# Attention beside an ELU feed-forward network: scores of two units by quarters of the array

## Chip, cores and metric

One Trainium2 chip, one NeuronCore. The metric is the device time of the whole kernel in microseconds (us), the median of several executions. Engines are named as in the profile: PE (TensorE matmul) and PEld (its weight loads), DVE (VectorE), ACT (ScalarE), POOL (GpSimd), SP (SyncE, which only issues transfers here).

## What is computed

The reference, cut to what matters (batch 4, 8 heads, 768 positions, head size 64, all float32):

```python
k_sum = k.reshape(B, H, nb, 32, D).max(axis=3)          # 24 blocks of 32 positions
v_sum = v.reshape(B, H, nb, 32, D).mean(axis=3)
scores_l = where(|i - j| < 16, scale * q @ k.T, -1e9)
scores_s = scale * q @ k_sum.T + log(32)
a = softmax(concat([scores_l, scores_s]))
x = (a @ concat([v, v_sum]))                            # as [3072 tokens, 512]
h = x @ w_in                                            # 512 -> 2048
out = where(h > 0, h, exp(min(h, 0)) - 1) @ w_out       # 2048 -> 512
```

## The kernel before

**Feed-forward.** The 3072 tokens are worked in 6 chunks of 512, and the 2048 hidden features in 16 strips of 128, so there are 96 slots, numbered n (chunk c = n // 16, strip f = n % 16). In each slot PE does `layer1(c, f)` (12 matmuls of 128x128 weights against 512 columns, L499) and then `layer2` of the slot before (12 matmuls of the same size, L527). Each product is split into a rounded and a remaining part (xh, xl and gh, gl), which is why there are three matmuls for each 128x128 block. Between the layers ACT takes the exponential (L505), DVE makes the ELU of it (L509, L510), ACT rounds it to gh (L516) and POOL makes the rest gl (L517).

**Attention.** A unit is a third of one batch's sequence (256 positions, four windows of 64) for one pair of heads. A window's 64 queries see 96 neighbouring keys (its own 64 and 16 on each side) and the 24 block maxima, 120 columns in all (`KC`). The first two thirds of batch 0 are done by `first_units()` ahead of the slots. The other 40 units u are spread over the slots of the chunks before the one that uses them, one unit in two slots. Chunk 0 holds units 0 to 7, chunks 1 to 4 hold units 8 to 39, chunk 5 holds none.

- `unit_scores(u)` (L459 to L463), in an even slot between the two layers: four matmuls, one for each window, on the whole array. The weights are `qbd`, a block-diagonal tile: the first head's 64x64 queries in rows and columns 0 to 63, the second head's in 64 to 127, zeros elsewhere. Two DMAs (L398) lay q there. Float32 matmuls leave two records each in the trace, so a unit shows x8.
- `lowest` (DVE, L130) adds the mask to four windows and finds the extremum, `exps` (ACT, L137) takes the exponentials and their sums, `normalize` takes reciprocals on DVE (L142, L143) and scales on POOL (L144).
- `unit_transposes(u)` (L149), at the end of the even slot after the scores' own: four transposes into PSUM, and an ACT copy to `pt` (L478).
- `unit_values(u)` (L156), at the end of the next odd slot: eight matmuls (x16 in the trace) of 120x64 weights, one for each window and head, the two heads in two column halves of the array. `take_x` then moves the result to xh on ACT (L169) and xl on DVE (L170).

**Order.** Chunk 0 runs with the order on every engine as written. From chunk 1 on, only PE and SP keep the written order (L639); the order on DVE, ACT and POOL is chosen when the program is built. PSUM has eight banks: two for h, four for the outputs of layer 2, and a0 and a1, which all of attention shares; `bank(c)` (L443) gives a0 in chunk 0 and then a0 and a1 in turn. `load_unit` (L393) brings a unit's q, keys and values by DMA from SP; q has two buffers, keys and values have one for each pair of heads. The 24 means of v are summed by `means` (L450), four matmuls in four column quarters of the array, three times in the run, and once by `sums` in `first_units` (L315).

Of the kernel before, what the change touches and what calls it, by code (L numbers as in the profile page):

```python
# [17 lines left out]
F32 = mybir.dt.float32  # L18
# [8 lines left out]
P = 128  # L27
# [3 lines left out]
QW = 64  # L31
KB = QW + 2 * E
UW = 4
UT = UW * QW
# [4 lines left out]
def attn_elu_ffn(ctx: ExitStack, tc: tile.TileContext, qT, kT, vT, v, w_in, w_out, out):  # L39
# [81 lines left out]

    ks_all, vs_all = {}, {}

    def lowest(th, s_ps, sm):

        mx = att.tile([P, UW, 1], F32, tag="mx", name="mx", bufs=4)
        for t in range(UW):
            w = th * UW + t
            m = mask[:, 0 if w == 0 else 2 if w == NTH * UW - 1 else 1, :]
            nc.vector.tensor_tensor_reduce(out=sm[:, t, :], in0=s_ps[:, t, :], in1=m, scale=-scale, scalar=3.0e38,  # L130
                                           op0=ALU.add, op1=ALU.min, accum_out=mx[:, t, :])
        return mx

# [12 lines left out]
    def transposes(sm, tag, bufs=1):  # L146
        t_ps = psum.tile([P, UW, P], F32, tag=tag, name="t_ps", bufs=bufs)
        for t in range(UW):
            nc.tensor.transpose(t_ps[0:KC, t, :], sm[:, t, :], ident)  # L149
        return t_ps  # L150

    def values(v_t, w0, pt, tag):
        o_ps = psum.tile([P, UT], F32, tag=tag, name="o_ps")
        for t in range(UW):
            for h in range(2):
                nc.tensor.matmul(o_ps[h * D:(h + 1) * D, t * QW:(t + 1) * QW],  # L156
                                 v_t[0:KC, w0 + t, h * D:(h + 1) * D], pt[0:KC, t, h * QW:(h + 1) * QW],
                                 start=True, stop=True)
        return o_ps

# [229 lines left out]

    units = [(third, p) for third in range(2, NTH * B) for p in range(NP)]

    def load_unit(u):  # L393
        third, p = units[u]
        b, th = divmod(third, NTH)
        q_t = qbd[u % 2]
        for h in range(2):
            nc.sync.dma_start(  # L398
                out=q_t[h * D:(h + 1) * D, :, h * D:(h + 1) * D],
                in_=qT[b, p, h * D:(h + 1) * D, th * UT:(th + 1) * UT].rearrange("d (t q) -> d t q", q=QW))  # L400
        lo = 1 if th == 0 else 0
        hi = UW - 1 if th == NTH - 1 else UW
        src = kT[b, p]
        nc.sync.dma_start(out=kw[p][:, lo:hi, 0:KB],
                          in_=bass.AP(tensor=src.tensor, offset=src.offset + (th * UW + lo) * QW - E,
                                      ap=[[S, P], [QW, hi - lo], [1, KB]]))
        vsrc = v[b, :, p * P:(p + 1) * P]
        nc.sync.dma_start(out=vw[p][0:KB, lo:hi, :],
                          in_=bass.AP(tensor=vsrc.tensor, offset=vsrc.offset + ((th * UW + lo) * QW - E) * row,
                                      ap=[[row, KB], [QW * row, hi - lo], [1, P]]))  # L410
        if th == 0:
            nc.sync.dma_start(out=kw[p][:, 0, E:KB], in_=src[:, 0:KB - E])
            nc.sync.dma_start(out=vw[p][E:KB, 0, :], in_=vsrc[0:KB - E, :])
            put_maxima(b, p)
        if th == NTH - 1:
            nc.sync.dma_start(out=kw[p][:, UW - 1, 0:KB - E], in_=src[:, S - KB + E:S])
            nc.sync.dma_start(out=vw[p][0:KB - E, UW - 1, :], in_=vsrc[S - KB + E:S, :])
# [20 lines left out]
        for i, n in enumerate(got):  # L438
            nc.vector.tensor_reduce(out=dst[:, p, i * m:(i + 1) * m], in_=n, axis=AX.X, op=op)

    banks = {"n": 0}

    def bank(c):  # L443

        if c == 0:
            return "a0"
        banks["n"] += 1
        return f"a{banks['n'] % 2}"

    def means(b, c):  # L450
        ps = psum.tile([P, P], F32, tag=bank(c), name="vsps")
        for p in range(NP):
            nc.tensor.matmul(ps[p * BLK:(p + 1) * BLK, :], vst_all[b][:, p, :], ident, start=True, stop=True,
                             tile_position=(0, p * BLK))
        return lambda: nc.scalar.mul(out=vs_all[b], in_=ps, mul=1.0 / BLK)
# [2 lines left out]

    def unit_scores(u, c):  # L459
        p = units[u][1]  # L460
        s_of[u] = psum.tile([P, UW, KC], F32, tag=bank(c), name="s")
        for t in range(UW):
            nc.tensor.matmul(s_of[u][:, t, :], qbd[u % 2][:, t, :], kw[p][:, t, :], start=True, stop=True)  # L463

    def unit_low(u):
        sm_of[u] = att.tile([P, UW, KC], F32, tag="sm", name="sm")
# [2 lines left out]
    def unit_exps(u, low):  # L469
        z_of[u] = exps(sm_of[u], low)  # L470

    def unit_norm(u):
        normalize(sm_of[u], z_of.pop(u))

    def unit_transposes(u, c):
        t_ps = transposes(sm_of.pop(u), bank(c))
        pt_of[u] = att.tile([P, UW, P], F32, tag="pt", name="pt", bufs=1)
        return lambda: nc.scalar.copy(out=pt_of[u][0:KC], in_=t_ps[0:KC])  # L478

    def unit_values(u, c):  # L480
        third, p = units[u]
        if third % 2 == 0 and p == 0:
            new_x(third // 2)
        o_ps = values(vw[p], 0, pt_of.pop(u), bank(c))
        return lambda: take_x(o_ps, third, p)


    gs = {}
# [73 lines left out]
    def slot_a(n, c):  # L562

        u, odd = divmod(n, 2)
        if not odd and u + 1 < len(units):
            unit_scores(u + 1, c)
            if u + 2 < len(units):
                load_unit(u + 2)
        for b, first in first_of.items():
            if n == 2 * first - 1:  # L570
                means(b, c)()
            p, late = divmod(n - (2 * first - 1), 2)
            if 0 <= p < NP and not late:
                put_means(b, p, vw[p])

    def slot_b(n, c):
        u, odd = divmod(n, 2)
        return (unit_values if odd else unit_transposes)(u, c) if u < len(units) else lambda: None

    def begin_next():  # L580

# [8 lines left out]
    with tc.manual_schedule(engines=set(engines.values())):  # L590
        late = first_units()

        sums_at = {2: [(1, 0)], 3: [(0, 0)], 4: [(1, 1)], 5: [(0, 1), (1, 2)], 6: [(1, 3)], 7: [(0, 2)], 8: [(0, 3)]}
        got = {}
        new_summaries(1)
        e = None
        this = begin_next()
        for n in range(NF):
            u, odd = divmod(n, 2)

            h_ps = layer1(0, n)
            next(this, None)
            ahead = begin_next()
            if n > 0:
                split(0, n - 1, e)
            next(this, None)
            if n > 0:
                evacuate()
            list(late)
            if not odd:  # L610
                unit_norm(u)
            for i, p in sums_at.get(n, []):
                summary(1, p, (kT, vT)[i], got.pop((i, p)))
            slot_a(n, 0)
            for i, p in sums_at.get(n + 2, []):
                got[i, p] = load_summary(1, p, (kT, vT)[i], spares[i][p])
            load_more(12 + 2 * n)

            late, this = this, ahead
            next(this, None)  # L620
            ahead = begin_next()
            e = exp_of(h_ps)
            next(this, None)
            list(late)
            if not odd:
                low = unit_low(u + 1)
            elu(e, h_ps)
            if odd:
                unit_exps(u + 1, low)
            if n > 0:  # L630
                layer2(0, n - 1)
            late, this = this, ahead
            evacuate = slot_b(n, 0)
        list(late)
        split(0, NF - 1, e)
        evacuate()
        unit_norm(NF // 2)

    with tc.manual_schedule(engines={engines["PE"], engines["SP"]}):  # L639
        for n in range(NF, NCH * NF):  # L640
            c, f = divmod(n, NF)
            u, odd = divmod(n, 2)
            h_ps = layer1(c, f)
            e = exp_of(h_ps)
            turn = elu(e, h_ps)
            split(c, f, e)
            slot_a(n, c)
            if not odd and u + 1 < len(units):
                unit_exps(u + 1, unit_low(u + 1))
                unit_norm(u + 1)  # L650
            for b, first in first_of.items():
                p = n - (2 * first - 8)
                if p == 0:
                    new_summaries(b)
                for q, src in ((p, kT), (p - 2, vT)):
                    if 0 <= q < NP:
                        got = load_summary(b, q, src)
                        with tc.issue_after(turn):
                            summary(b, q, src, got)
            layer2(*divmod(n - 1, NF))  # L660
            slot_b(n, c)()
        layer2(NCH - 1, NF - 1)
# [37 lines left out]
```

## Time and profile before

| | us |
|---|---|
| median of 3 runs | 657.42 (657.16 to 658.16) |
| the profiled execution | 658.07 |
| its span, first to last instruction | 656.3 |
| PE busy | 639.7 (97%) |
| ACT, DVE, POOL busy | 275.6, 265.7, 245.3 |
| mean granted clock of PE | 0.99 of full speed |

A row of the timeline gives the start of a group of instructions, the time from its first start to its last end, the engine, the line, what is written and read, the tile of weights (rows*columns), the moving operand and the count. Starts are the safe part of a matmul's row: its end is modelled and overlaps the next one's start, so what a matmul costs is read from one start to the next.

### The profile page before, as it was taken

How to read it: one execution, taken by the hardware profiler on the slowest of the kernel's cores; microseconds unless marked ns; L12 is line 12 of the kernel's file. 1: busy time of each engine (PE TensorE's matmuls, PEld its weight loads, DVE VectorE, ACT ScalarE, POOL GpSimd, SP SyncE). 2: the span in 40 equal slices, each digit the busy share in tenths (PEclk: the TensorE clock that was granted, in tenths of full speed). 3: DMA queues.
4: the chain of work that ended last, by engine and by line, in shares of the span. 5: the costliest groups of instructions: out<-in, count | busy, mean ns of one | idle time of the engine just before them, and what ended most of it. 6: DMA issues, size and time to landing. Idle time of an engine off the chain costs nothing.

```text
span 656.3 us, 10774 instructions
## 1 busy us (share of the span) xinstructions
PE 639.7 (97%) x3916; PEld 523.8 (80%) x3916; DVE 265.7 (40%) x856; ACT 275.6 (42%) x750; POOL 245.3 (37%) x263
## 2 busy tenths in 40 slices
PE   8859999999999999999999999999999999999997
PEld 7648878888888878888888888888888888888885
DVE  7868887633224533322233543222322231322222
ACT  6757667644334333343344333433443343322222
POOL 5768989843222322232223232322232222222221
PEclk9969999999999999999999999999999999999999
DMA  9999965114122514121112551211321100100001
GB/s 315 208 317 351 308 212 167 33 36 125 32 56 80 151 34 134 36 60 38 32 35 72 171 137 38 70 32 33 97 64 31 32 1 1 64 1 1 0 1 64
DMA packets 86324, 60.24 MB, mean 92 GB/s; under 512 B 46464, under 2 KB 78464, under 8 KB 86272
## 3 DMA queue, kind: packets, MB, share of 16 engines
q1 hardware_dynamic: 82960, 53.66, 29.4%
q10 hardware_dynamic: 3312, 5.90, 2.4%
q8 instruction: 31, 0.51, 0.3%
q14 instruction: 21, 0.17, 0.1%
HBM read 52.46 MB, written 6.29 MB: 90 GB/s over the span
## 4 chain that ended last, share of the span: by engine, by line
PE 94%; DMA 2%; DVE 2%; ACT 1%; POOL 0%; SPq 0%; issue 0%; DVEq 0%
PE h L499 41%; PE o L527 40%; PE s L463 5%; PE o_ps L156 4%; PE t_ps L149 3%; DMA v<-in_v_dram 1%; DMA raw_w<-in_w_in_dram 1%; DMA raw_w<-in_w_out_dram 1%; DVE sm L130 1%; PE idle L227 1%; ACT sm L137 0%; PE s L290 0%; DVE sh L110 0%; DVE cv L113 0%; POOL raw_w L103 0%; DVE ks L276 0%
## 5 line engine op out<-in xcount | busy, mean ns | idle before, releaser
L499 PE MATMUL h<-xh,w 128*128 128x512 f32 x768 | 262.8, 403 | 0.0
L517 POOL TENSOR_TENSOR gl<-e,gh 128x512 fp32r<-128x512 f32 x96 | 123.9, 1290 | 205.3 <-issue 109.6
L527 PE MATMUL o<-w,gh 128*128 128x512 f32 x768 | 196.4, 394 | 0.0
L499 PEld LDWEIGHTS h<-xh,w 128*128 128x128 f32 x768 | 145.3, 189 | 31.2
L527 PEld LDWEIGHTS o<-w,gh 128*128 128x128 f32 x768 | 141.2, 188 | 28.2 <-issue 0.6
L499 PE MATMUL h<-xl,w 128*128 128x512 f32 x384 | 150.9, 393 | 0.0
L509 DVE TENSOR_SCALAR e<-e 128x512 f32<-128x512 f32 x96 | 45.1, 469 | 254.2 <-ACT e L505 254.1
L505 ACT ACTIVATE e<-h 128x512 f32<-128x512 f32 x96 | 57.4, 598 | 210.9 <-PE h L499 210.0
L144 POOL TENSOR_TENSOR sm<-sm,z 128x480 f32<-128x480 f32 x48 | 47.5, 990 | 157.0 <-ACT gh L516 130.9
L527 PE MATMUL o<-w,gl 128*128 128x512 f32 x384 | 105.3, 389 | 0.0
L516 ACT CAST gh<-e 128x512 fp32r<-128x512 f32 x96 | 59.0, 615 | 72.9 <-DVE e L510 71.6
L137 ACT ACTIVATE sm<-sm,mx 128x120 f32<-128x120 f32 x192 | 73.5, 385 | 26.5 <-DVE mx L130 26.5
L527 PEld LDWEIGHTS o<-w,gl 128*128 128x128 f32 x384 | 72.0, 188 | 15.2 <-POOL gl L517 0.2
L499 PEld LDWEIGHTS h<-xl,w 128*128 128x128 f32 x384 | 72.9, 190 | 13.0
L510 DVE SCALAR_TENSOR_TENSOR e<-h,e 128x512 f32<-128x512 f32 x96 | 66.2, 690 | 2.2
L170 DVE TENSOR_TENSOR xl<-o_ps,xh 128x256 fp32r<-128x256 f32 x48 | 20.0, 423 | 61.4 <-ACT xh L169 61.4
L118 POOL TENSOR_TENSOR w<-cv,w 128x512 fp32r<-128x512 f32 x32 | 42.4, 1325 | 6.7 <-ACT w L117 5.8
L463 PEld LDWEIGHTS s<-kw,qbd 128*128 128x128 f32 x320 | 41.8, 191 | 3.7 <-DVE xl L170 0.7
L130 DVE CUSTOM_DVE_ANT_0 sm<-s,mask 128x120 f32<-128x120 f32 x192 | 42.2, 277 | 1.8 <-PE s L463 1.7
L463 PE MATMUL s<-kw,qbd 128*128 128x120 f32 x320 | 41.9, 274 | 0.6 <-DVE xl L170 0.6
L149 PE MATMUL t_ps<-ident,sm 128*120 128x128 f32 x192 | 29.3, 276 | 8.5 <-DVE mx L130 6.8
L137 ACT ACTIVATION_READ_ACCUMULATOR sm<-sm,mx 128x1 f32 x192 | 36.1, 188 | 0.0
(66 smaller groups left out, 361.1 us busy)
## 6 DMA issues: line engine op xcount, KB each, us to landing
raw_w<-in_w_in_dram SPq DMA_DIRECT2D x16, 512.0 KB, 6.3
raw_w<-in_w_out_dram SPq DMA_DIRECT2D x16, 512.0 KB, 6.1
qbd<-in_qT_dram SPq DMA_DIRECT2D x80, 64.0 KB, 2.3
out_dram<-ot ACTq DMA_DIRECT2D x20, 256.0 KB, 3.8
kw<-in_kT_dram SPq DMA_DIRECT2D x28, 144.0 KB, 5.9
vw<-in_v_dram SPq DMA_DIRECT2D x28, 144.0 KB, 2.9
n<-in_kT_dram SPq DMA_DIRECT2D x16, 192.0 KB, 2.5
n<-in_vT_dram SPq DMA_DIRECT2D x16, 192.0 KB, 2.6
```

The lines of the kernel that those rows point to most:

```text
L130: nc.vector.tensor_tensor_reduce(out=sm[:, t, :], in0=s_ps[:, t, :], in1=m, scale=-scale, scalar=3.0e38, op0=ALU.add, op1=ALU.min, accum_o ...
L137: nc.scalar.activation(out=sm[:, t, :], in_=sm[:, t, :], func=AF.Exp, bias=mx[:, t, :], scale=-1.0, accum_out=z[:, t, :])
L144: nc.gpsimd.tensor_tensor(out=sm, in0=sm, in1=z.broadcast_to([P, UW, KC]), op=ALU.mult)
L149: nc.tensor.transpose(t_ps[0:KC, t, :], sm[:, t, :], ident)
L463: nc.tensor.matmul(s_of[u][:, t, :], qbd[u % 2][:, t, :], kw[p][:, t, :], start=True, stop=True)
L499: nc.tensor.matmul(h_ps, w[:, a, cols], bb[:, cc, :], start=(k == 0), stop=(k == 3 * NCC - 1))
L505: nc.scalar.activation(out=e, in_=h_ps, func=AF.Exp)
L509: nc.vector.tensor_scalar(out=e, in0=e, scalar1=1.0, scalar2=-1.0, op0=ALU.min, op1=ALU.add)
L510: top = nc.vector.scalar_tensor_tensor(out=e, in0=h_ps, scalar=0.0, in1=e, op0=ALU.max, op1=ALU.add)
L516: nc.scalar.copy(out=gh, in_=e)
L517: nc.gpsimd.tensor_tensor(out=gl, in0=e, in1=gh.bitcast(F32), op=ALU.subtract)
L527: nc.tensor.matmul(o_acc[c][s], a[:, s * P:(s + 1) * P], w[:, bb, :], start=first and f == 0, stop=last and f == NF - 1)
```

## The change

Chunk 0 stays as it was, but that it no longer scores unit 8. From there on, units go by twos, and one pair has four slots. `scores_of_two(u)` runs at the end of slot n = 2u - 1, after `layer2`: 16 matmuls with 64x64 weights, each on a quarter of the array: the row half is the head, the column half is the window's parity. Each head has a PSUM bank of its own (a0, a1). q is loaded as it lies, in one DMA, without the zeros. The transposes of the two units follow at the ends of the next two slots, and `values_of_two` does the values of both in one run at the end of the last slot. The masks of the first and last window now hold for one half of the partitions, so two halves are copied over once. `pt` gets two buffers. The number of operations on DVE, ACT and POOL for a unit is the same.

The diff, without the lines that only pass names on:

```diff
     def lowest(th, s_ps, sm, two=False):
...
+            s_t = s_ps[t % 2][:, t // 2, :] if two else s_ps[:, t, :]
+            nc.vector.tensor_tensor_reduce(out=sm[:, t, :], in0=s_t, in1=m, scale=-scale, scalar=3.0e38,
...
+    def values(v_t, w0, pt, tag=None, o_ps=None, two=False):
...
+                                 pt[0:KC, t // 2 * 2 + h, t % 2 * QW:(t % 2 + 1) * QW] if two else
+                                 pt[0:KC, t, h * QW:(h + 1) * QW],
...
+    def q_flat(u):
+        return qbd[u % 2].rearrange("p t k -> p (t k)")[:, 0:UT]
...
+        if u >= NF // 2:
+            nc.sync.dma_start(out=q_flat(u), in_=qT[b, p, :, th * UT:(th + 1) * UT])
+        for h in range(2 if u < NF // 2 else 0):
...
+    def scores_of_two(u):
+        s_ps = [psum.tile([P, UW, KC], F32, tag=f"a{h}", name="s") for h in range(2)]
+        for k in range(2):
+            for i in range(UW // 2):
+                for h, g in ((0, 0), (1, 0), (0, 1), (1, 1)):
+                    rows = slice(h * D, (h + 1) * D)
+                    w = 2 * i + g
+                    nc.tensor.matmul(s_ps[h][g * QW:(g + 1) * QW, 2 * k + i, :],
+                                     q_flat(u + k)[rows, w * QW:(w + 1) * QW], kw[units[u + k][1]][rows, w, :],
+                                     start=True, stop=True)
+        for k in range(2):
+            sm_of[u + k] = att.tile([P, UW, KC], F32, tag="sm", name="sm")
+            low = lowest(units[u + k][0] % NTH, [s[:, 2 * k:2 * k + 2, :] for s in s_ps], sm_of[u + k], two=True)
+            unit_exps(u + k, low)
+            unit_norm(u + k)
...
-        t_ps = transposes(sm_of.pop(u), bank(c))
-        pt_of[u] = att.tile([P, UW, P], F32, tag="pt", name="pt", bufs=1)
+        t_ps = transposes(sm_of.pop(u), "a1" if c > 0 and u % 2 else "a0")
+        pt_of[u] = att.tile([P, UW, P], F32, tag="pt", name="pt")
...
+    def values_of_two(u, c):
...
+        o_ps = psum.tile([P, 2, UT], F32, tag="a0", name="o_ps")
+        for i in range(2):
+            values(vw[p + i], 0, pt_of.pop(u + i), o_ps=o_ps[:, i, :], two=True)
+        for i in range(2):
+            take_x(o_ps[:, i, :], third, p + i)
...
     def slot_a(n, c):
-        if not odd and u + 1 < len(units):
-            unit_scores(u + 1, c)
-            if u + 2 < len(units):
-                load_unit(u + 2)
+        if c == 0 and not odd:
+            if u + 1 < NF // 2:
+                unit_scores(u + 1, c)
+            load_unit(u + 2)
...
     def slot_b(n, c):
         u, odd = divmod(n, 2)
-        return (unit_values if odd else unit_transposes)(u, c) if u < len(units) else lambda: None
+        if c == 0:
+            return (unit_values if odd else unit_transposes)(u, c)
+        u, part = divmod(n + 1, 4)
+        u *= 2
+        if part == 0 and u < len(units):
+            scores_of_two(u)
+            for w in (u + 2, u + 3):
+                if w < len(units):
+                    load_unit(w)
+        elif part in (1, 2) and u < len(units):
+            unit_transposes(u + part - 1, c)()
+        elif part == 3 and u < len(units):
+            values_of_two(u, c)
+        return lambda: None
...
-        unit_norm(NF // 2)
+        nc.vector.tensor_copy(out=mask[QW:P, 0, :], in_=mask[QW:P, 1, :])
+        nc.vector.tensor_copy(out=mask[0:QW, 2, :], in_=mask[0:QW, 1, :])
 
     with tc.manual_schedule(engines={engines["PE"], engines["SP"]}):
+        slot_b(NF - 1, 1)
         for n in range(NF, NCH * NF):
...
             slot_a(n, c)
-            if not odd and u + 1 < len(units):
-                unit_exps(u + 1, unit_low(u + 1))
-                unit_norm(u + 1)
```

## Rows read from the trace of the kernel before

**Rows 1.** The page: busy time of the engines, and PE's granted clock.

```profile
PE 639.7 (97%) x3916; PEld 523.8 (80%) x3916; DVE 265.7 (40%) x856; ACT 275.6 (42%) x750; POOL 245.3 (37%) x263
PEclk9969999999999999999999999999999999999999
```

**Rows 2.** Timeline of PE, two slots of chunk 2: start us, us, engine, line, operation.

```profile
299.69 0.50 PE L499 MATMUL h<-xh,w 128*128 128x512 f32 x1
...
302.55 1.05 PE L463 MATMUL s<-kw,qbd 128*128 128x120 f32 x8
303.36 2.07 PE L527 MATMUL o<-w,gh 128*128 128x512 f32 x8
...
306.17 0.60 PE L149 MATMUL t_ps<-ident,sm 128*120 128x128 f32 x4
306.52 0.48 PE L499 MATMUL h<-xh,w 128*128 128x512 f32 x1
...
312.17 0.69 PE L156 MATMUL o_ps<-pt,vw 120*64 120x64 f32 x16
312.79 0.50 PE L499 MATMUL h<-xh,w 128*128 128x512 f32 x1
```

**Rows 3.** Timeline of PE, the last slots with attention, one without scores.

```profile
549.05 0.50 PE L499 MATMUL h<-xh,w 128*128 128x512 f32 x1
...
554.99 0.47 PE L499 MATMUL h<-xh,w 128*128 128x512 f32 x1
...
561.24 0.50 PE L499 MATMUL h<-xh,w 128*128 128x512 f32 x1
```

**Rows 4.** Timeline of PE, two slots of chunk 5, which has no attention.

```profile
583.13 0.39 PE L499 MATMUL h<-xh,w 128*128 128x512 f32 x1
...
594.01 0.39 PE L499 MATMUL h<-xh,w 128*128 128x512 f32 x1
```

**Rows 5.** Timeline of PE, whole-array transposes and then L315 by column quarters.

```profile
15.07 1.09 PE L149 MATMUL t_ps<-ident,sm 128*120 128x128 f32 x8
16.09 1.52 PE L315 MATMUL vsps<-vn,mean 128*32 128x128 f32 x48
```

**Rows 6.** The same, its first 30 ns alone.

```profile
16.09 0.32 PE L315 MATMUL vsps<-vn,mean 128*32 128x128 f32 x4
```

**Rows 7.** Timeline of PE, 64x64 weights on two quarters, and its first 8 ns alone.

```profile
9.66 1.51 PE L290 MATMUL s<-kn,qn 64*64 64x96 f32 x32
...
9.66 0.28 PE L290 MATMUL s<-kn,qn 64*64 64x96 f32 x2
```

**Rows 8.** Timeline of PE, values of five units in a run, and its first pair alone.

```profile
25.67 2.55 PE L156 MATMUL o_ps<-pt,v 120*64 120x64 f32 x80
...
25.67 0.28 PE L156 MATMUL o_ps<-pt,v 120*64 120x64 f32 x2
```

**Rows 9.** Timeline of DVE, ACT and POOL after the scores of rows 2.

```profile
303.78 0.28 DVE L130 CUSTOM_DVE_ANT_0 sm<-s,mask 128x120 f32<-128x120 f32 x1
...
304.10 0.40 ACT L137 ACTIVATE sm<-sm,mx 128x120 f32<-128x120 f32 x1 [0.69 <-DVE mx L130]
...
305.63 0.61 ACT L516 CAST gh<-e 128x512 fp32r<-128x512 f32 x1
305.76 0.17 DVE L142 TENSOR_SCALAR z<-z 128x4 f32<-128x4 f32 x1 [0.48 <-ACT sm L137]
...
306.31 0.99 POOL L144 TENSOR_TENSOR sm<-sm,z 128x480 f32<-128x480 f32 x1 [5.93 <-ACT gh L516]
```

**Rows 10.** Groups by line, 142 to 560 us: busy us, mean ns, idle before them.

```profile
L505 ACT ACTIVATE e<-h 128x512 f32<-128x512 f32 x64 | 38.3, 598 | 148.8 <-PE h L499 148.8
...
L510 DVE SCALAR_TENSOR_TENSOR e<-h,e 128x512 f32<-128x512 f32 x64 | 44.1, 689 | 1.1
...
L509 DVE TENSOR_SCALAR e<-e 128x512 f32<-128x512 f32 x64 | 27.3, 427 | 185.4 <-ACT e L505 185.4
```

**Rows 11.** Timeline where chunk 0 ends: values of unit 7 and their way to x.

```profile
142.51 0.69 PE L156 MATMUL o_ps<-pt,vw 120*64 120x64 f32 x16
143.12 0.73 PE L499 MATMUL h<-xh,w 128*128 128x512 f32 x2
143.24 0.37 ACT L169 CAST xh<-o_ps 128x256 fp32r<-128x256 f32 x1 [1.80 <-PE o_ps L156]
143.65 0.42 DVE L170 TENSOR_TENSOR xl<-o_ps,xh 128x256 fp32r<-128x256 f32 x1 [3.04 <-ACT xh L169]
```

More of the change, by code (lines that the diff above doesn't have):

```diff
@@ L122, in attn_elu_ffn, with lowest @@
     ks_all, vs_all = {}, {}
-    def lowest(th, s_ps, sm):
+    def lowest(th, s_ps, sm, two=False):
         mx = att.tile([P, UW, 1], F32, tag="mx", name="mx", bufs=4)
@@ L128, in lowest @@
             w = th * UW + t
+            if two:
+                w = w // 2 * 2 if th == 0 else w // 2 * 2 + 1
             m = mask[:, 0 if w == 0 else 2 if w == NTH * UW - 1 else 1, :]
-            nc.vector.tensor_tensor_reduce(out=sm[:, t, :], in0=s_ps[:, t, :], in1=m, scale=-scale, scalar=3.0e38,
+            s_t = s_ps[t % 2][:, t // 2, :] if two else s_ps[:, t, :]
+            nc.vector.tensor_tensor_reduce(out=sm[:, t, :], in0=s_t, in1=m, scale=-scale, scalar=3.0e38,
                                            op0=ALU.add, op1=ALU.min, accum_out=mx[:, t, :])
@@ L150, in transposes @@
         return t_ps
-    def values(v_t, w0, pt, tag):
-        o_ps = psum.tile([P, UT], F32, tag=tag, name="o_ps")
+    def values(v_t, w0, pt, tag=None, o_ps=None, two=False):
+        if o_ps is None:
+            o_ps = psum.tile([P, UT], F32, tag=tag, name="o_ps")
         for t in range(UW):
@@ L156, in values @@
                 nc.tensor.matmul(o_ps[h * D:(h + 1) * D, t * QW:(t + 1) * QW],
-                                 v_t[0:KC, w0 + t, h * D:(h + 1) * D], pt[0:KC, t, h * QW:(h + 1) * QW],
+                                 v_t[0:KC, w0 + t, h * D:(h + 1) * D],
+                                 pt[0:KC, t // 2 * 2 + h, t % 2 * QW:(t % 2 + 1) * QW] if two else
+                                 pt[0:KC, t, h * QW:(h + 1) * QW],
                                  start=True, stop=True)
@@ L396, in load_unit @@
         q_t = qbd[u % 2]
-        for h in range(2):
+        if u >= NF // 2:
+            nc.sync.dma_start(out=q_flat(u), in_=qT[b, p, :, th * UT:(th + 1) * UT])
+        for h in range(2 if u < NF // 2 else 0):
             nc.sync.dma_start(
@@ L439, in summary @@
             nc.vector.tensor_reduce(out=dst[:, p, i * m:(i + 1) * m], in_=n, axis=AX.X, op=op)
[L441 to L448, printed above, removed]
     def means(b, c):
-        ps = psum.tile([P, P], F32, tag=bank(c), name="vsps")
+        ps = psum.tile([P, P], F32, tag="a1" if c > 0 else "a0", name="vsps")
         for p in range(NP):
@@ L460, in unit_scores @@
         p = units[u][1]
-        s_of[u] = psum.tile([P, UW, KC], F32, tag=bank(c), name="s")
+        s_of[u] = psum.tile([P, UW, KC], F32, tag="a0", name="s")
         for t in range(UW):
             nc.tensor.matmul(s_of[u][:, t, :], qbd[u % 2][:, t, :], kw[p][:, t, :], start=True, stop=True)
+    def scores_of_two(u):
[13 more added lines that the diff above has]
+            unit_norm(u + k)
     def unit_low(u):
@@ L483, in unit_values @@
             new_x(third // 2)
-        o_ps = values(vw[p], 0, pt_of.pop(u), bank(c))
+        o_ps = values(vw[p], 0, pt_of.pop(u), "a0")
         return lambda: take_x(o_ps, third, p)
+    def values_of_two(u, c):
+        third, p = units[u]
+        if third % 2 == 0 and p == 0:
+            new_x(third // 2)
+        o_ps = psum.tile([P, 2, UT], F32, tag="a0", name="o_ps")
[4 more added lines that the diff above has]
+        return lambda: None
     gs = {}
@@ L577, in slot_b @@
         u, odd = divmod(n, 2)
-        return (unit_values if odd else unit_transposes)(u, c) if u < len(units) else lambda: None
+        if c == 0:
[11 more added lines that the diff above has]
+            values_of_two(u, c)
+        return lambda: None
     def begin_next():
@@ L624, in attn_elu_ffn @@
             list(late)
-            if not odd:
+            if not odd and u + 1 < NF // 2:
                 low = unit_low(u + 1)
             elu(e, h_ps)
-            if odd:
+            if odd and u + 1 < NF // 2:
                 unit_exps(u + 1, low)
```

## The prediction

> **What bounds the kernel now.** I read the page first. PE is busy for 97% of the span and no other engine for more than 42%, and its clock is granted in full but for a stretch early in chunk 0 [rows 1], which the change doesn't touch. So the question is what PE's own instructions cost in the slots, and whether the new order makes PE wait.
>
> For the first I laid slots with and without attention side by side in PE's timeline, from the first layer 1 matmul of one slot to that of the next. A slot of chunk 5, with no attention, takes (594.01 - 583.13) / 2 = 5.44 us [rows 4]. An even slot with scores and transposes takes 306.52 - 299.69 = 6.83, and the odd slot with values 312.79 - 306.52 = 6.27 [rows 2]. The last even slot, which has transposes but no scores any more, takes 554.99 - 549.05 = 5.94, and the odd slot behind it 6.25 [rows 3]. By differences: scores cost 6.83 - 5.94 = 0.89 us, transposes 5.94 - 5.44 = 0.50, values 6.27 - 5.44 = 0.83. All of it, 2.22 us a unit, is on the path: PE shows no idle time in these slots. The slots repeat at these lengths from chunk 1 to chunk 4, so 32 units are touched, which makes 16 pairs.
>
> **Part 1, the scores.** Removed: for a pair, 2 x 0.89 = 1.78 us. Added: 16 matmuls, 32 records, of 64x64 weights against 120 columns on four quarters in turn. No row shows four quarters of 64x64 at once, so I bound them. Four column quarters do run together: the four records of one round of L315 all start within 30 ns [rows 6], and 48 records, 12 rounds of 4, take (1.52 - 0.32) / 11 = 0.109 us a round [rows 5, 6]. One whole-array transpose with as many columns takes as long as such a round (1.02 us for eight from 15.07 to 16.09, about 0.11 for each, the switch included) [rows 5], so the four don't slow each other. Two 64x64 quarters with 96 columns take (1.51 - 0.28) / 15 = 0.082 us a round [rows 7]. Both are 0.85 ns a column, so 120 columns make 0.102 us a round. If four quarters go at once there are 8 rounds, 0.82 us; if only two go at once there are 16, 1.64 us. I take 0.82: L315 is the nearest row to four at once, and it shows no loss. What it doesn't have is two row halves that write the same partitions, here in two banks.
>
> Second, a run on parts of the array has a fixed cost at its ends. Values show it: in the run of 80 records one round of two takes (2.55 - 0.28) / 39 = 0.058 us [rows 8], so a unit's eight rounds are 0.47 us, of its 0.83: the fixed part is 0.36 us. For the scores on the whole array it is hardly there (the first starts right behind layer 1). So scores of two cost 0.82 + 0.36 = 1.18 us, with 1.0 to 2.0 as ends, and the pair gains 1.78 - 1.18 = 0.60.
>
> The Trainium skill (TensorEngine Tiling (Array Packing), Key Properties) says that a change of tiling mode drains the array; the trace agrees, by the 0.36 us above. It also speaks against the full factor: in TensorE: Matmul & The Clock Gate (Part 3, Measured speedup vs the span model) four row tiles came to 3.07 times one, not 4. By it a round would be about 1.3 times as long, an estimate from that page, and the kernel some 4 us slower than my sum. No run here shows that yet.
>
> **Part 2, the values.** Their records stay as many, 16 rounds of two for a pair, 0.93 us, but in one run instead of two, so the fixed 0.36 us is paid once. The pair gains 0.36 and has 1.29 for 1.66 us.
>
> **Part 3, the transposes.** They stay, at 2 x 0.50 us.
>
> **Part 4, what else moves.** DVE, ACT and POOL keep their operations, but two units' worth come at once, after the scores, and the transposes of the first follow after one slot. I checked each wait that PE meets.
>
> - Transposes of the first unit wait for its scaled exponentials. In the trace from PE's next matmul after the scores (303.36) to the end of the scaling (306.31 + 0.99) it is 3.94 us [rows 2, 9]. PE reaches the transposes after a layer 1 and a layer 2, 5.44 us. The cover is 1.5 us, so this costs nothing. The second unit has one more slot.
> - Layer 2 of the next slot waits for gh and gl. ACT's exponential of h can be held up behind the second unit's, which takes 305.63 - 304.10 = 1.53 us [rows 9]; layer 2 comes a whole layer 2 and layer 1 later, more than 5 us after h is ready, and exp, ELU and rounding sum to 0.60 + 0.43 + 0.69 + 0.61 = 2.33 us [rows 9, 10]. Nothing again.
> - Banks a0 and a1: scores wait for `take_x` of the pair before, one slot earlier; transposes wait for `lowest` of both units, eight times 0.2 us after the scores. Both are covered by a slot.
> - SP: the loads of the next pair stand behind the scores of this one, since q's two buffers are read there, but they have four slots, over 20 us, to land. Nothing that PE needs sooner is queued behind them. There is one DMA for q instead of two.
> - Once, at the end of chunk 0, there is a wait that isn't covered: the scores of unit 8 need a0, which holds the values of unit 7 until xl is taken, at 143.65 + 0.42 = 144.07, and PE is through with them at 143.12 [rows 11]. That is 1.0 us, with 0 to 1.5 as ends. The two mask copies on DVE are no larger than its other operations and PE waits for none of them directly.
>
> **The sum.** A pair gains 0.60 + 0.36 = 0.96 us, 16 pairs 15.4, less 1.0 at the boundary: 14.4 us. Against the profiled execution, 658.07 us, that is 643.7; it lies 0.65 above the median of the runs, and against the median, 657.42, it is 643.0 us, which I predict. The fixed part of the scores is the least certain term: its ends are 0.08, what the whole-array scores pay (0.89 less the 303.36 - 302.55 = 0.81 from their first start to the next matmul [rows 2]), which would give 638.5 us, and twice 0.36 (rival 3). I take 0.36, since values too run on parts of the array; half of the way to either end is some 2 to 3 us.
>
> **The rivals.**
>
> 1. Row halves don't go together with each other where they write the same partitions, so only two quarters run at once. Then scores of two are 1.64 + 0.36 = 2.00 us, 0.22 dearer than before, the pair gains 0.14, and the kernel comes to 657.4 - 2.2 + 1.0 = 656.2 us. For it: no row shows such a pair. Against: two quarters in different row halves do start within 8 ns in L290 [rows 7]. Its milder form, rounds between 0.102 and 0.205 us, lies between; a third of the way is 8 x 0.034 x 16 = 4.4 us, 647.4.
> 2. The new order makes PE wait (the slower side). The order on DVE and POOL is fixed when the program is built. If the reciprocals of the first unit (L142) are put behind the ELU of the next slot, its scaling comes late: from the end of the scores 0.42 to `lowest`, 0.32 to the exponentials, 2 x 1.53 for both units, 0.60 for the exponential of h, 1.12 for the ELU, 0.4 for the reciprocals, 0.99 on POOL, with handovers 7.1 us [rows 9, 10]. PE is there after 5.44, so it would wait 1.65 us in each pair, 26 us in all: 669 us. It decides the sign from a wait of 0.9 us a pair on. Against: in the trace L142 stands right behind its own exponentials [rows 9], and the second unit's come later in the written order.
> 3. The quarters do as expected but switching into and out of them costs twice the fixed part: 16 x 0.36 = 5.8 us less, 648.8 us.
>
> **How the numbers follow.** The forecast, 640.5 to 645.5 us, has 70%; the milder form of rival 1 and rival 3 together 12% (645.5 to 650); rival 1 in full 8% (656.2, of which half within the bound of no change); rival 2 10%, most of it with a wait above 0.9 us. The range 640 to 649.5 us holds the forecast and the second case. About 0.2%, 1.3 us, is what a measurement of this kernel can tell from no change: faster 0.87, same 0.05, slower 0.08.
>
> **What would show it.** After the change an odd slot with scores of two should take 5.44 + 1.18 = 6.6 us, the two with transposes 5.94, the one with values 6.73, together 25.2 for 26.2 us. Rounds of four records 0.10 us apart in the new scores line show part 1; rounds of two, or four records spread evenly over 0.2 us, show rival 1. Idle time of PE ahead of the transposes with POOL's scaling as releaser shows rival 2. Wrong would be the whole reading if slots get shorter and the end doesn't, for PE is the only thing that I count.

## The result and the profile after

The changed kernel takes 649.56 us (648.33 to 650.17), the kernel before, measured beside it, 657.79. The ratio is 0.9865, 95% interval 0.985 to 0.988: faster by 1.35%, 8.2 us. The forecast was 643.0 with 640.0 to 649.5 as range. The time stands 0.06 us above the end of that range; the forecast was made against 657.42 us, and 0.9865 of that is 648.5, inside it. The sign holds, and the gain is little more than half of the 14.4 us that the sum gave. Ratios compare executions in the fast state alone; of the kernels below only e5 had others, four of ten, so its ratio is not that of the medians shown.

The page of the changed kernel: busy time of the engines, and PE's granted clock in 40 slices (to be held against [rows 1]).

```profile
PE 627.5 (97%) x4172; PEld 507.9 (78%) x4172; DVE 269.8 (42%) x858; ACT 275.3 (42%) x750; POOL 249.4 (38%) x263
PEclk9969999999999999999999899999999999999999
```

PE has 12 us less to do, more than the span has lost, and one slice in the middle, which was 9, is an 8. So something makes PE wait, and it happens in few places. The slots say where. First a usual pair, slots 40 to 43, from PE's timeline (start us, us; to be held against [rows 2]):

```profile
296.92 0.50 PE L531 MATMUL h<-xh,w 128*128 128x512 f32 x1
...
302.89 0.48 PE L531 MATMUL h<-xh,w 128*128 128x512 f32 x1
...
308.80 0.47 PE L531 MATMUL h<-xh,w 128*128 128x512 f32 x1
...
314.44 1.15 PE L161 MATMUL o_ps<-pt,vw 120*64 120x64 f32 x32
315.52 0.50 PE L531 MATMUL h<-xh,w 128*128 128x512 f32 x1
...
321.19 1.05 PE L476 MATMUL s<-kw,qbd 64*64 64x120 f32 x32
322.17 0.50 PE L531 MATMUL h<-xh,w 128*128 128x512 f32 x1
```

Two slots with transposes take 5.97 and 5.91 us, the one with values of two 6.72, the one with scores of two 6.65: 25.25 us for a pair, where the prediction had 25.2 and the kernel before 26.18. The first 30 ns of those scores alone show the first round:

```profile
321.19 0.33 PE L476 MATMUL s<-kw,qbd 64*64 64x120 f32 x4
```

Four records start together, and a round takes (1.05 - 0.33) / 7 = 0.103 us.

Now the slots that are not usual. PE's waits from 142 to 560 us (who waited for whom: us in all, times, longest):

```profile
PE o L559 <- ACT ot L580: 1.5, 2, 1.2
PE t_ps L153 <- POOL sm L148: 1.2, 1, 1.2
PE s L476 <- DVE xl L177: 0.9, 1, 0.9
PE o L559 <- DVE ot L580: 0.2, 1, 0.2
```

The third is the wait for a0 at the end of chunk 0, foreseen at 1.0 us. The second is in slot 28, which takes 7.38 instead of 5.97 us. The first and the fourth are in slot 49, the second of chunk 3, which takes 10.25 instead of 5.91. The account, from one execution of each kernel: 16 pairs at 26.18 - 25.25 = 0.93 give 14.9 us. Off this go 1.4 in slot 28, 4.3 in slot 49 and 0.2 in the next, some 0.8 at the boundary, and 0.4 in slots 0 and 1, where the work is as before and whose length wanders from one profile to another (18.2 to 20.9 us for both). That leaves 7.8; the span is 656.3 - 648.4 = 7.9 us shorter.

**Slot 28.** The timeline around the transposes of unit 14, DVE and what comes of it (idle time before an instruction in brackets):

```profile
220.31 0.55 DVE L451 TENSOR_REDUCE vst<-n 128x12 f32<-128x384 f32 x1 [1.98 <-DMA n<-in_vT_dram]
...
220.78 0.27 DVE L134 CUSTOM_DVE_ANT_0 sm<-s,mask 128x120 f32<-128x120 f32 x1
...
222.49 0.55 DVE L451 TENSOR_REDUCE vst<-n 128x12 f32<-128x384 f32 x1 [1.43 <-DMA n<-in_vT_dram]
...
222.96 0.28 DVE L134 CUSTOM_DVE_ANT_0 sm<-s,mask 128x120 f32<-128x120 f32 x1
...
226.13 0.65 PE L153 MATMUL t_ps<-ident,sm 128*120 128x128 f32 x4 [1.19 <-POOL sm L148]
```

The order on DVE is fixed, and it puts two halves of a reduction for the means of v (batch 2, slot 27) ahead of and between the windows of unit 14. DVE waits for their loads. The first window comes at 220.78 instead of 0.42 us after the scores (219.16), the second 2.2 us later, and the cover of 1.5 us is gone.

**Slots 48 and 49.** SP, DVE, ACT and PE at the start of chunk 3:

```profile
353.12 12.63 SPq L442 DMA_DIRECT2D n<-in_kT_dram  x6
...
355.48 1.18 DVE L451 TENSOR_REDUCE ks<-n 128x12 f32<-128x384 f32 x2 [2.78 <-DMA n<-in_kT_dram]
...
356.07 0.59 ACT L580 COPY ot<-o 128x512 f32<-128x512 f32 x1 [1.81 <-DVE ks L451]
...
356.70 1.52 PE L559 MATMUL o<-w,gh 128*128 128x512 f32 x4 [0.31 <-ACT ot L580]
...
358.75 0.59 ACT L580 COPY ot<-o 128x512 f32<-128x512 f32 x1 [0.24 <-DMA out_dram<-ot]
...
359.39 0.73 PE L559 MATMUL o<-w,gh 128*128 128x512 f32 x2 [1.16 <-ACT ot L580]
```

The loads for the maxima of batch 3 are issued at 353.12, behind the ten transfers of two units, which SP issued from 347.14 on (the expectation of e4 says nine). Their tiles `n` share two buffers (tag `cv`) with the output tiles `ot`, so the copy of chunk 2's output waits for the reduction, the next copies wait for the first ones' way out, and layer 2 of chunk 3 waits for its four banks. Then the clock falls. Busy time by stage (span us, PE, PEld, DVE, ACT, POOL, granted clock, share of DMA, GB/s):

```profile
353.39:363.64 10.25, 8.49 (x32) 5.64 (x30) 3.52 (x6) 2.97 (x5) 2.83 (x3) 0.85 0.50 171
360.50:363.90 3.40, 3.40 (x11) 2.70 (x12) 0.23 (x1) 0.00 (x0) 1.28 (x1) 0.51 0.61 196
```

PE stands idle for 10.25 - 8.49 = 1.8 us of slot 49, and after that it runs 3.4 us at half speed (1.2 GHz), which costs about another 1.7, an estimate: half of the 3.4. The two make 3.5 of the 4.3 us; the rest counts as busy in these rows and isn't split further here.

### The profile page after: what moved, and what is told of

It reads as the page before. It is cut to its first block, busy times and chain, and to the rows that moved or that the text cites. A ratio compares the mean times of both kernels' runs of the same rounds, so it can differ in the third digit from the quotient of the medians.

```text
span 648.4 us, 11246 instructions
## 1 busy us (share of the span) xinstructions
PE 627.5 (97%) x4172; PEld 507.9 (78%) x4172; DVE 269.8 (42%) x858; ACT 275.3 (42%) x750; POOL 249.4 (38%) x263
## 4 chain that ended last, share of the span: by engine, by line
PE 89%; DMA 4%; DVE 3%; ACT 1%; POOL 1%; SPq 1%; issue 1%; ACTq 0%; DVEq 0%; POOLq 0%
PE h L531 40%; PE o L559 39%; PE o_ps L161 3%; PE t_ps L153 3%; PE s L476 2%; DMA raw_w<-in_w_in_dram 2%; PE s L466 1%; DVE sm L134 1%; DMA kn<-in_kT_dram 1%; ACT sm L141 1%; DMA n<-in_vT_dram 1%; POOL sm L148 0%; DMA n<-in_kT_dram 0%; DVE e L542 0%; DVE ks L283 0%
## 5 line engine op out<-in xcount | busy, mean ns | idle before, releaser
L559 PEld LDWEIGHTS o<-w,gh 128*128 128x128 f32 x768 | 143.2, 188 | 33.5 <-ACT ot L580 2.3
L148 POOL TENSOR_TENSOR sm<-sm,z 128x480 f32<-128x480 f32 x48 | 50.6, 1053 | 59.0 <-DVE z L147 46.4
L153 PEld LDWEIGHTS t_ps<-ident,sm 128*120 128x120 f32 x192 | 23.4, 139 | 17.1 <-POOL sm L148 11.2
L498 ACT COPY pt<-t_ps 120x512 f32<-120x512 f32 x40 | 23.4, 586 | 21.4 <-PE t_ps L153 21.3
```

The lines of the kernel that those rows point to most:

```text
L148: nc.gpsimd.tensor_tensor(out=sm, in0=sm, in1=z.broadcast_to([P, UW, KC]), op=ALU.mult)
L559: nc.tensor.matmul(o_acc[c][s], a[:, s * P:(s + 1) * P], w[:, bb, :], start=first and f == 0, stop=last and f == NF - 1)
```

## The experiments

All kernels are edits of the changed kernel, but e8, which is the changed kernel itself, run again. Slots are measured in PE's timeline from the first layer 1 matmul to the next one's. "4 to 94" is the time from the first layer 1 matmul of slot 4 to that of slot 94, which leaves the wandering start out. Slots are from one execution, medians from several. The measured ratio has its own kernel before beside it (658.83 us for e1 to e3, 658.82 for e4 to e7, 658.10 for e8 to e10). Slots 28 and 49 hold other stalls in e1 to e3 than in the changed kernel, so there a usual pair tells more than the total.

| kernel | median us | ratio to before (95%) | pair (slots 40 to 43) | slot 28 | slot 31 | slot 49 | 4 to 94 |
|---|---|---|---|---|---|---|---|
| before | 657.79 | | 26.18 | | | | 574.7 |
| changed | 649.56 | 0.9865 (0.985 to 0.988) | 25.25 | 7.38 | 7.23 | 10.25 | 566.4 |
| e1 whole array | 659.64 | 1.0013 (1.0003 to 1.0022) | 25.80 | 5.89 | 7.86 | 11.91 | 575.7 |
| e2 single values | 653.91 | 0.9927 (0.991 to 0.9943) | 25.60 | 7.08 | 7.23 | 9.11 | 570.4 |
| e3 two quarters | 656.00 | 0.9961 (0.9946 to 0.9975) | 25.71 | 6.22 | 7.69 | 8.64 | 570.8 |
| e4 loads later | 647.58 | 0.9836 (0.9815 to 0.9857) | 25.25 | 7.27 | 7.23 | 7.39 | 564.2 |
| e5 own buffers | 656.88 | 0.9923 (0.9888 to 0.9958) | 25.25 | 8.69 | 7.23 | 6.39 | 569.5 |
| e6 sums moved | 644.63 | 0.9791 (0.9767 to 0.9815) | 25.25 | 5.97 | 8.71 | 5.91 | 561.9 |
| e7 and h bank | 644.43 | 0.9794 (0.9765 to 0.9822) | 25.25 | 5.97 | 7.63 | 5.91 | 560.5 |
| e8 changed, again | 648.49 | 0.9854 (0.984 to 0.9869) | 25.25 | 6.93 | 7.23 | 9.72 | 566.1 |
| e9 output tiles apart | 646.19 | 0.9815 (0.9792 to 0.9839) | 25.25 | 6.94 | 7.23 | 7.18 | 562.7 |
| e10 sums early, h bank | 643.29 | 0.9772 (0.9751 to 0.9792) | 25.25 | 5.97 | 7.23 | 5.91 | 560.5 |

### Where the gain comes from: e1, e2, e3

**e1: the scores of two on the whole array.**

```diff
-                for h, g in ((0, 0), (1, 0), (0, 1), (1, 1)):
-                    ... 64x64 of q_flat, bank of the head
+            for t in range(UW):
+                nc.tensor.matmul(s_ps[k][:, t, :], qbd[(u + k) % 2][:, t, :], kw[...][:, t, :], start=True, stop=True)
```

> The pair order and the values of two stay; the scores go back to the whole array with block-diagonal q, a bank for each unit (a0, a1), two DMAs for q, and the mask halves are not copied. Theory (the quarters are what saves time in the scores): a slot with scores grows from 6.65 to 5.44 + 2 x 0.89 = 7.2 us, 16 pairs by 0.6 us, 9.6 us in all, so about 659 us against 649.6 of the changed kernel. Rival (the gain of the scores comes from going by two, in one run, not from the quarters): within 2 us of 649.6.

Measured 659.64 us. PE's timeline, one run of scores in it:

```profile
323.66 1.94 PE L471 MATMUL s<-kw,qbd 128*128 128x120 f32 x16
325.37 0.48 PE L525 MATMUL h<-xh,w 128*128 128x512 f32 x1
```

The slot with scores takes 7.28 us, 0.63 more than with quarters, and nothing else in a usual pair moves by over 0.1. The gain of the scores lies in the quarters; going by two gives none of it.

**e2: the values one unit at a time.**

```diff
         elif part in (1, 2) and u < len(units):
             unit_transposes(u + part - 1, c)()
+            if part == 2:
+                values_of_one(u, c)
         elif part == 3 and u < len(units):
-            values_of_two(u, c)
+            values_of_one(u + 1, c)
```

> The quarter scores stay; the values of the two units are done apart, the first unit's right behind the second unit's transposes, the second unit's at the end of the pair's last slot. Theory (a fixed 0.36 us is paid at the ends of each run on parts of the array): the pair is 0.36 us longer, 16 pairs 5.8 us, so about 655.4 us; the slot with transposes and values 6.7 us, the slot with the second unit's values 6.25. Rival (the records alone cost, the run's ends nothing, and the gain of 0.36 us lay in something else): within 1.5 us of 649.6.

Measured 653.91 us. Its slots, values of each unit in turn:

```profile
309.82 0.69 PE L161 MATMUL o_ps<-pt,vw 120*64 120x64 f32 x16
310.44 0.50 PE L524 MATMUL h<-xh,w 128*128 128x512 f32 x1
...
316.10 0.69 PE L161 MATMUL o_ps<-pt,vw 120*64 120x64 f32 x16
316.72 0.50 PE L524 MATMUL h<-xh,w 128*128 128x512 f32 x1
```

The pair is 25.60 - 25.25 = 0.35 us longer, as expected (0.36). The total is 1.5 us under the expected one, mainly because of slot 49. It holds a unit's values here and would take 6.70 us, so its 9.11 is a stall of 2.4 us for the base's 4.3. The fixed cost of a run on parts of the array is shown.

**e3: only two quarters at a time.**

```diff
-                for h, g in ((0, 0), (1, 0), (0, 1), (1, 1)):
+        for pair in (((0, 0), (1, 1)), ((1, 0), (0, 1))):   # outermost
+                    for h, g in pair:
```

> The same 16 quarter matmuls of a pair in another order: first all on the two quarters of one diagonal, then all on the two of the other, so that only two quarters can be busy at once. Theory (a round of quarters takes 0.102 us however many are in it): 16 rounds for 8, a slot with scores 0.82 us longer, 7.5 for 6.65 us, 13.1 us in all, about 662.7 us, which is slower than before. Rival (what bounds the run is the number of records or of weight loads, 32 at some 0.026 us, not how many quarters are busy): no change, within 2 us of 649.6.

Measured 656.00 us: neither. The slot with scores is 7.11 us, 0.46 longer, where 0.82 and 0 were expected. Four windows of PE's timeline: the whole run, its first 20 ns, its first 0.47 us, and the 30 ns around 299.35.

```profile
298.87 1.51 PE L477 MATMUL s<-kw,qbd 64*64 64x120 f32 x32
...
298.87 0.32 PE L477 MATMUL s<-kw,qbd 64*64 64x120 f32 x2
...
298.87 0.73 PE L477 MATMUL s<-kw,qbd 64*64 64x120 f32 x10
...
299.12 0.54 PE L477 MATMUL s<-kw,qbd 64*64 64x120 f32 x8
```

The run starts with rounds of two, five of them, ten records, in the first 0.47 us. Then the pairs come closer: eight records start from 299.12 to 299.36, which is one pair more than rounds of 0.103 us allow. The rows don't name the quarter, but the first diagonal's two are busy with their round, so the extra pair can only be the second diagonal's, six records ahead of its turn. The whole run is 1.51 - 0.32 = 1.19 us longer than its first round, instead of 15 x 0.102 = 1.53. So quarters that are free are fed ahead of the program's order, as far as the rows' spacing tells. What the experiment was for still follows: how many quarters are busy sets the time, not the number of records (32 in both).

### Where the rest of the gain went: e4 to e9

**e4: the loads of the next pair behind the transposes, a unit at a time.**

```diff
             scores_of_two(u)
-            for w in (u + 2, u + 3):
-                if w < len(units):
-                    load_unit(w)
         elif part in (1, 2) and u < len(units):
             unit_transposes(u + part - 1, c)()
+            if u + part + 1 < len(units):
+                load_unit(u + part + 1)
```

> The loads of the next pair are not issued together behind the scores, but one unit's behind each of the two slots with transposes. Cause looked for: the stall of 4.3 us in slot 49, at the start of chunk 3. Theory A (nine transfers of two units stand on SP ahead of the loads for the block maxima, 353.1 us, so these come late, and the output tiles that share their two buffers with them come late): slot 49 is 5.9 us again, slot 28 keeps its wait of 1.4 us, the time is some 645.2 us. Rival B (the sharing of the two buffers is enough by itself, whatever stands on SP): slot 49 stays at about 10 us, the time at 649 to 650.

Measured 647.58 us; slot 49 is 7.39, between the two. The reductions of slot 48 come at 351.79, 0.8 us ahead of slot 49 instead of 2.1 us into it, and PE's clock doesn't fall. But the output copies are still late:

```profile
351.79 1.00 DVE L451 TENSOR_REDUCE ks<-n 128x12 f32<-128x384 f32 x2
...
353.32 0.59 ACT L580 COPY ot<-o 128x512 f32<-128x512 f32 x1
...
358.09 0.73 PE L559 MATMUL o<-w,gh 128*128 128x512 f32 x2 [0.57 <-DVE ot L580]
```

The backlog on SP makes the stall larger, and is not all of it. Slot 28 stays (7.27). Slot 52, after the same reductions of batch 3, is 6.92; it was 5.97 in the changed kernel's trace, but 6.54 in e2 and 6.66 in e8, so this isn't e4's doing alone.

**e5: the blocks for maxima and means in the idle halves of the q tiles, in three parts.**

```diff
-        parts = 1 if spare else 2
+        parts = 1 if spare else 3
-                n = ffn.tile([P, m, BLK], F32, tag="cv", name="n", bufs=2)
+                n = (idle half of qbd[0] and qbd[1] in turn)
```

> The blocks of k and v for maxima and means are loaded into the halves of the q tiles that are idle from chunk 1 on, in three parts instead of two, and no longer into the two buffers that the output tiles use. The loads of a pair stay together on SP. Theory B (the sharing of the buffers makes the output tiles wait in slot 48): slot 49 is near 5.9 us, the time some 645 us; slot 28 (a wait for a load of v on DVE, between the rows of the first unit) stays or moves a little. Theory A (late loads by the backlog on SP) alone, with the order of DVE fixed so that output copies stand behind the late maxima: slot 49 stays above 8 us and the time above 647.

Measured 656.88 us, with executions from 647.65 to 658.68. In this kernel the third part is loaded over the first before that is reduced, so the maxima and means are not the reference's, and the reductions wait for all three parts. That makes slots 28 and 52 longer (8.69 and 9.53 us), and the total says nothing. Slot 49 is 6.39 us: without the shared buffers it is nearly free of the stall, though the loads stand behind the same backlog. Since the reductions too are timed otherwise here, e9 asks the same in a cleaner way.

**e6: no reduction in the first slot of a chunk, none in a slot with scores.**

```diff
-                for q, src in ((p, kT), (p - 2, vT)):
-                    if 0 <= q < NP:
+                for q, src in {1: [(0, kT)], 2: [(1, kT), (0, vT)], 4: [(2, kT), (1, vT)],
+                               5: [(3, kT), (2, vT)], 6: [(3, vT)]}.get(p, []):
```

> The loads and reductions for block maxima and means keep buffers and queues, but none is left in the first slot of a chunk (slot 48) and none in a slot with scores of two (27, 51): they go by slots 1, 2, 4, 5, 6 of the eight. Theory (both stalls are collisions of these reductions with something in the same slot, output tiles in 48 and the rows of the first unit in 27): slots 28 and 49 are 5.97 and 5.92 us, 1.4 + 4.3 us less, about 643.9 us. Rival (the two stalls come from the pair's loads, whatever the reductions do): slots 28 and 49 stay long, 648 us or more.

Measured 644.63 us. Slots 28 and 49 are 5.97 and 5.91 us: both stalls are gone, with buffers, queues and the pair's loads as they were. But slot 31 is 8.71 instead of 7.23, since the last reduction for v now comes just ahead of the means that use it. PE's waits from 142 to 600 us:

```profile
PE vsps L456 <- DVE vst L451: 1.0, 1, 1.0
PE s L476 <- DVE xl L177: 0.9, 1, 0.9
```

**e7: that, and unit 7's values in a bank of h.**

```diff
-        o_ps = values(vw[p], 0, pt_of.pop(u), "a0")
+        last = psum.tile([P, UT], F32, tag="h", name="o_ps", bufs=2) if u == NF // 2 - 1 else None
+        o_ps = values(vw[p], 0, pt_of.pop(u), "a0", o_ps=last)
```

> As the run before it, and the values of unit 7, the last of chunk 0, go to a bank of layer 1 (h) instead of a0. Theory (the scores of unit 8 waited 0.9 us for a0 at the end of chunk 0): PE doesn't wait there, slot 15 is 7.3 instead of 8.2 us, the time 0.9 us below the run before it, about 643.0. Rival (layer 1 of slot 16 or 17 then waits for that bank, or for x of unit 7): the same time as the run before it, within 0.3 us.

Measured 644.43 us, 0.2 under e6, which the intervals don't tell apart. The wait for a0 is gone, but slot 15 goes from 8.24 to 7.80 only, where 7.48 would be its work (5.44 + 1.21 + 0.83). Four records of the scores now stand ahead of the last part of layer 2, so there is one more change between quarters and the whole array. The place is where two parts of the program meet; that the build reorders PE's work there is likely, but not shown:

```profile
138.90 0.42 PE L476 MATMUL s<-kw,qbd 64*64 64x120 f32 x4
139.25 1.20 PE L560 MATMUL o<-w,gl 128*128 128x512 f32 x4
140.38 0.69 PE L161 MATMUL o_ps<-pt,vw 120*64 120x64 f32 x16
141.00 1.04 PE L476 MATMUL s<-kw,qbd 64*64 64x120 f32 x28
```

**e8: the changed kernel again**, as a base for e9 and e10.

> The changed kernel as it is, as the base of the two runs beside it. Theory (the stalls of slots 28 and 49 are set by orders and queues that are fixed, not by chance): slot 28 at 7.0 to 7.4 us and slot 49 above 8 us again, 648 to 650 us. Rival (they come from one execution): both slots near 5.9 us and some 644 us.

Measured 648.49 us, slot 28 at 6.93, slot 49 at 9.72. The stalls are in the order, not in one execution; their size varies by half a microsecond. Slot 52, the counterpart of slot 28 in batch 3, is 6.66 here and was 5.97 in the first trace, so this stall comes in some executions only.

**e9: the output tiles in the buffers of pt.**

```diff
-                    ot = ffn.tile([P, DO], F32, tag="cv", name="ot", bufs=2)
+                    ot = att.tile([P, DO], F32, tag="pt", name="ot")
```

> The four output tiles of a chunk's last strip use the two buffers of pt, idle in that slot, instead of the two that the loads for maxima and means use; the loads stay as in the changed kernel. Theory (in slot 48 the output tiles wait for buffers that late maxima still hold): slot 49 is 5.9 to 6.5 us for 10.25, slot 28 keeps its 7.2 to 7.4, about 645.5 us. Rival (the output copies come late because DVE works the late maxima ahead of them, whatever buffer they use): slot 49 stays above 7.3 us, 647 us or more.

Measured 646.19 us; slot 49 is 7.18, 2.5 us less than in e8 and 1.3 more than a usual one. Again both have a part. What is left, in its timeline:

```profile
356.04 1.01 DVE L451 TENSOR_REDUCE ks<-n 128x12 f32<-128x384 f32 x2 [3.42 <-DMA n<-in_kT_dram]
356.97 0.68 DVE L580 COPY ot<-o 128x512 f32<-128x512 f32 x1
...
357.70 0.73 PE L559 MATMUL o<-w,gh 128*128 128x512 f32 x2 [0.96 <-DVE ot L580]
```

With a buffer of its own the last output copy still stands behind the reductions in DVE's order, and DVE waits 3.4 us there for loads that SP issued late.

### A faster version: e10

```diff
+                for q, src in {1: [(0, kT)], 2: [(1, kT), (0, vT)], 4: [(1, vT), (2, vT)],
+                               5: [(3, vT), (2, kT)], 6: [(3, kT)]}.get(p, []):
```

with e7's bank for unit 7.

> Reductions moved as in the earlier run, but with the means of v done one slot sooner (slots 1, 2, 4, 5, 6 hold k; k and v; v and v; v and k; k), and unit 7's values in a bank of h. Theory (what was left is the wait of the means for the last reduction in slot 31): slot 31 is 7.23 us, no wait of PE above 0.3 us from slot 16 on, about 643.5 us. Rival (two loads of v in one slot only move the wait to another slot): 644.4 or more, with one slot above its kind by 0.5 us or more.

Measured 643.29 us (ratio 0.9772): the lowest median of all, 2.3% under the kernel before and below the changed kernel's interval; the intervals of e6 and e7 overlap with its own. The trace shows no wait of PE's matmuls for another engine from slot 16 up to 600 us, but slot 30 is 7.13 us, 0.4 over its kind. A weight load waits there. ACT, DVE and PEld around slot 30, which starts at 230.22:

```profile
227.41 0.60 ACT L538 ACTIVATE e<-h 128x512 f32<-128x512 f32 x1 [2.23 <-PE h L532]
...
229.94 0.55 DVE L451 TENSOR_REDUCE vst<-n 128x12 f32<-128x384 f32 x1 [1.93 <-DMA n<-in_vT_dram]
...
231.00 0.55 DVE L451 TENSOR_REDUCE vst<-n 128x12 f32<-128x384 f32 x1 [0.51 <-DMA n<-in_vT_dram]
...
231.92 0.69 DVE L543 SCALAR_TENSOR_TENSOR e<-h,e 128x512 f32<-128x512 f32 x1
...
232.65 0.62 ACT L549 CAST gh<-e 128x512 fp32r<-128x512 f32 x1 [4.64 <-DVE e L543]
...
233.32 1.69 PEld L560 LDWEIGHTS o<-w,gh 128*128 128x128 f32 x8 [0.53 <-ACT gh L549]
```

The exponential is done at 228.0, but the ELU stands on DVE behind two reductions that wait for their loads, so gh, the weights of layer 2, comes late. It is the collision of slot 28 once more with another victim, a small form of the expectation's rival. From slot 4 to slot 94 e10 gains 14.2 us on the kernel before, where the prediction's sum was 14.4 after 1.0 taken off at the boundary.

## Why the prediction was right, and where it was not

**Part 1, scores.** Right. 1.18 us for a pair was forecast; the slot gives 6.65 - 5.44 = 1.21. A round of four takes 0.103 us for 0.102, and e1 gives 0.63 for the forecast gain of 0.60. Rival 1 (row halves that write the same partitions exclude each other) is out: four records start within 30 ns. The 3.07 that the Trainium skill has for four row tiles (TensorE: Matmul & The Clock Gate, Part 3, Measured speedup vs the span model) is not what this kernel shows; a round of four quarters takes 0.86 ns a column, where a round of two took 0.85 [rows 7], and the 4 us that it would have cost are not there.

**Part 2, values.** Right: 6.72 - 5.44 = 1.28 us for 1.29, and e2 gives the fixed part as 0.35 for 0.36. Rival 3, that quarters switch more dearly, is out by the same slots: 1.21 less 0.82 of rounds leaves 0.39.

**Part 3.** Right: 0.53 and 0.47 for 0.50 each.

**Part 4, the boundary.** Right in kind: a wait of 0.9 us for a0, forecast at 1.0.

**Part 4, the other waits.** Here the prediction failed, in two of its four bullets, and both times for the same reason: each wait was checked in a usual pair, and the slots in which the reductions for the next batch run were never looked at.

- "This costs nothing", of the transposes of the first unit. True in 15 of 16 pairs of that profile (14 in e8's); in slot 28 two reductions stand among the unit's windows on DVE and eat the cover. That is rival 2's mechanism (the order on DVE is fixed at build time), with another instruction in the way and once or twice instead of 16 times; the rival's deciding point of 0.9 us a pair was not approached. Before the change the same reductions were harmless (slot 28 took 6.83 us there, as its neighbours): a unit's transposes came two slots after its scores.
- "Nothing that PE needs sooner is queued behind them", of the loads on SP. It is false in slot 48: the loads for the maxima are queued there, and on them hang, through two shared buffers and DVE's order, the output copies and the banks of layer 2. e4 and e9 each take a part of the stall away (10.25 and 9.72 in the base, 7.39 and 7.18 with them), e6 all of it. So it is a collision: without the reductions in that slot there is no stall, and the backlog and the shared buffers each make it larger. That DVE's order is the third part is read from the rows and wasn't tested by itself. The half clock behind it, 3.4 us, is a part that no sum of waits had; in e3, where the clock stayed full, slot 49 was 2.7 us over its kind instead of 4.3.

Both together are 1.4 + 4.3 + 0.2 = 5.9 us of the 6.2 by which the gain was missed; a pair's gain of 0.93 us for 0.96 is 0.5 more, less 0.2 at the boundary. e10, which removes the two stalls and more than half of the boundary's, lands at 643.29.

**The range.** That the time came out at its upper end is luck. The forecast itself, 640.5 to 645.5 us, was missed, and the part above it was there for a milder rival 1 and for rival 3, which the slots rule out. Rival 2, the only one on waits, was priced as a wait in each of 16 pairs.

## What to carry to other kernels

When an engine is full, cost its work slot by slot, by differences between slots with and without a part: here that gave each term within 0.03 us. Then look for waits in the rare slots, not in the usual one: list what else uses the queue, the buffers and the engine order that the change loads more heavily, and check each in the slot where it runs. A stall can cost more than its idle time: slot 49 with 1.8 us of it was 4.3 us longer, a half clock included.

## What the runs showed of the hardware

- Four 64x64 quarters, in pairs that write the same partitions in two banks, run together without loss: 0.103 us for a round of four with 120 columns, 0.86 ns a column, as for two quarters and for four column quarters before [rows 5 to 7].
- A run on parts of the array costs 0.35 to 0.39 us at its two ends, whether 64x64 quarters or 120x64 halves. Scores on the whole array have little of it (0.08 us a run by rows 2, as the prediction worked out).
- Matmuls are fed to free quarters ahead of the program's order: in e3 the second diagonal started when 10 of the 16 records of the first had. The Trainium skill (TensorE: Matmul & The Clock Gate, Part 3, The mechanism) has matmuls start and end strictly in the program's order; e3 doesn't agree.
- Behind the stall of slot 49 PE's clock was granted at half (1.2 GHz) for 3.4 us in the changed kernel (0.51 from 360.5 to 363.9 us) and again in e8, and for 6.8 us in e1, but not in e2, e3, e4 and e9, where it stays at full speed (2.4 GHz) in that slot. The amount of idle time in the slot doesn't tell the two kinds apart: it is 1.8 us in the changed kernel and 1.4 in e8, but 1.7 in e3 and 1.4 in e2. What does is not shown. Slot 49 of e8 and of e3 (columns as in the stage rows above, the granted clock third from the end):

```profile
350.81:360.54 9.73, 8.30 (x32) 5.62 (x30) 3.52 (x6) 2.98 (x5) 2.83 (x3) 0.84 0.49 172
357.71:366.35 8.64, 6.96 (x32) 4.58 (x29) 3.47 (x6) 2.98 (x5) 2.84 (x3) 1.00 0.50 173
```
